# A new written-out order for all engines of a fused attention and squared-ReLU kernel, with load gates and PSUM banks named in the list

## The chip, the core and the metric

The kernel runs on one core of one Trainium2 chip. The metric is the device time of one execution in microseconds (us), as the median of the runs shown. The core has TensorE (PE in the profile, with its weight loads listed apart as PEld), VectorE (DVE), ScalarE (ACT), GpSimd (POOL) and SyncE (SP). Here POOL's instructions are nearly all starts of loads that convert float32 to float16 on the way, and SP's are starts of DMA transposes and of stores.

## The reference

Four batches of eight heads, 768 positions, head size 64, go through an attention in which each position sees eight global positions and the last 96 ones, with a distance bias. The result, 3072 tokens of 512 numbers, goes through a two-layer network with a squared ReLU.

```python
scores = scale * np.matmul(q, k.transpose(0, 1, 3, 2))
is_global = pos[None, :] < int(n_global)                 # n_global = 8
is_local = (rel >= 0) & (rel < int(n_local))             # n_local = 96
dist = np.where(is_global & ~is_local, float(n_local), np.abs(rel).astype(np.float32))
scores = scores + (-slopes[:, None, None] * dist[None, :, :])
scores = np.where(is_global | is_local, scores, -1000000000.0)
...
a = a / (np.sum(a, axis=-1, keepdims=True) + 1e-09)
x = np.matmul(a, v).transpose(0, 2, 1, 3).reshape(B * S, H * D)
h = np.maximum(x @ w_in, 0.0)                            # w_in 512 x 2048
out = h * h @ w_out                                      # w_out 2048 x 512
```

## The kernel before

**Tiling.** The tokens are cut into eight halves of 384 (three tiles of 128); half 0 and half 1 belong to batch 0, and so on. The heads go in four pairs, a = 0 to 3. Everything between the loads and the stores is float16, with float32 sums in PSUM, which has eight banks of 128 x 512.

**Attention.** For each half, q and k come in as tokens x features (`sq`, `sk`), are turned so that features lie on the partitions, and scored (`score_unit`, L691 holds its matmuls: 64 rows of weights, 128 columns). ACT takes the exponential (L704), DVE multiplies by a mask that holds bias and window (`weigh`, L728), PE multiplies with v (`attend`, L752; the 65th column gives the sum of the weights), and DVE divides (`norm`, L762, result `tm`). `tm` is turned into `xt`, features x tokens. For halves 0 and 1, "the opening", that work goes tile by tile and the turning is done by PE; half 2's q and k are turned by PE (`turn`, L629). For halves 3 to 7 SP turns q and k by DMA transposes (`turn_by_dma`, L647), and for halves 2 to 7 it turns `tm` into `xt` by four more, one for each pair (`to_x_by_dma`, L777).

**The network.** Layer 1 goes plainly over output tiles of 128 (`layer1`, L797), or, for part of the hidden width of halves 2 to 7, in groups of seven products of half size in place of eight (`layer1_group`, L900). These use sums and differences of quarters of w_in (`in_mix`) and of `xt` (`x_mix`, DVE, L878), and keep partial sums out of PSUM for a while (`hold`, a copy by ACT or DVE, printed as L336 or L338) to add them to later products (L958). ReLU and square follow on ACT or DVE (L822 and L836, L966 to L1000). Layer 2 goes plainly (`layer2`, L1052) or, for most of the tokens, two token tiles at a time in seven products (`layer2_pair`, L1138), with mixed weights `w_mix` and mixed hidden tiles `mixed` (`token_sum`, DVE, L1103). Its products share two or three PSUM banks named "a", "f" and "c". A product that adds to a bank waits until the copy (`hold`) or the hand-out (`hand_out`, L1200) of the bank's former content is done. Each pair's two rows of the output are stored by SP, 256 KB at a time; the last pair's last row is stored in pieces by SP and ACT.

**Loads.** POOL starts 128 KB loads of q, k and v tiles (L472), and 512 KB loads of quarters of w_in (L534) and of w_out (L541). No more than eight of its loads are outstanding in the trace. For halves 2 and up the loads of q and k into the staging tiles wait until the half before has been turned. For halves above 3, the first load of k is also placed behind both turning transposes of the half before, through a manual dependence (`behind`).

**The order.** The functions above only append operations to lists of `Plan`: PE's jobs (index p), loads (index l) and everything else (index a, d, s or g in the order, one common numbering). A job of p is a whole group of matmuls, such as one product or one score unit. The order in which all operations are then issued is the string `ORDER`, read by `by_table`: each word is a letter for the engine (p PE, l POOL's loads, a ACT, d DVE, s SP, g POOL) and an index. The same operation can stand as a or d, if both engines can do it. An engine works its words off in the order of the string, and waits where the data or the buffer of an instruction isn't ready. `run` also holds a small model of the engines' times. By it, it picks the PSUM bank of each PE job (the idle bank that came free first, `idle_banks`), and it works out how many filler matmuls on zeros stand ahead of some jobs in the first 24 us (`warm`, `spare`).

Of the kernel before, what the change touches and what calls it, by code (L numbers as in the profile page):

```python
# [41 lines left out]
AFTER = [0, 0, 0, 0, 0, 0, 0, 0]  # L42
# [10 lines left out]
ORDER = """d1 g2 a4 p0 a6 s8 d12 a0 s10 d17 l3 d13 l1 a18 a16 a19 l2 d21 d20 a27 l5 a26 d14 a22 d15 d3 a28 d5  # L53
p10 l4 a25 d9 p5 a30 d146 l0 a24 p1 a11 p2 d7 l6 a23 p3 l10 a32 d31 a33 d34 p6 l9 a29 d36 p7 a39 p11
d35 l7 p8 a46 p4 d43 p9 a41 l8 d37 p13 d44 a40 p12 d45 a47 l11 p14 d38 p16 a42 p15 d48 l13 p17 d51
a49 p19 p24 a52 l12 d55 p20 d64 p22 a50 p23 d58 l14 a53 p34 d56 p30 a60 p25 d71 p28 l16 p21 a81 d59
p26 d57 a82 l18 p27 d69 d67 p31 a65 d68 p18 a61 p29 l15 d72 p36 p32 a54 d70 p35 l19 a86 d66 p33 a73
d85 p39 d62 p40 l17 a74 a77 d76 p37 l21 d91 a78 p41 l20 d79 d63 p38 d83 l23 a101 d75 d84 p45 l22 a89
a87 d96 p44 l27 p47 a92 d80 p48 d107 a97 l29 d111 p46 a98 p52 l28 p43 a93 d110 p53 p42 d105 l30 d119
p55 d120 p50 l24 p59 a122 a88 d90 d99 a102 p51 l25 d106 a103 d94 p49 a116 a128 d108 p67 d100 a129  # L60
d95 a117 d112 p57 a104 p65 d125 p54 p58 d121 d189 p63 p61 p62 a132 d126 a109 p60 a114 d135 d118 a113
d115 p56 a127 d205 d191 a133 p74 a130 p72 a169 d138 p73 a165 d131 p77 d123 a166 p69 a167 p75 d156
d147 a157 p70 p71 d134 a158 p82 d159 l34 a162 d168 p81 a163 d186 l26 a170 p83 a142 p68 l31 d174 a139
d160 d149 p84 l35 a184 a164 d208 p64 a187 d124 l33 d161 a171 d148 a144 p85 l32 d272 a143 d206 p88
d207 l36 p89 d201 p79 d151 p86 a198 a178 d204 p91 d152 a195 a199 d188 p76 d202 a136 d150 p87 a172
d200 a179 p90 a196 d180 a193 p80 d153 a209 p78 s194 l37 p66 d155 a175 d203 a137 p95 d210 p92 a176
d223 a173 p94 d197 s224 l38 a185 d177 p100 a211 l39 d236 a181 s216 p93 a140 d237 p96 a182 p103 d238
s217 p97 d183 a244 a240 d221 a141 p102 d219 a222 d154 p106 s220 d213 d225 p98 p104 d239 s226 p99
d227 d228 p105 a234 d214 s229 d145 a218 d243 p101 l44 d245 d246 p107 l43 s215 d212 a241 d190 p109
l40 p110 p108 p111 a255 d192 l42 a251 p112 a256 d258 l45 a248 d257 p113 l41 a249 d230 d232 a252 p118  # L70
d259 p114 a273 d253 s260 l46 p116 d254 p115 a261 p120 d231 d250 l47 a262 p122 a264 p124 l48 s235
d280 p123 a265 d263 p131 a268 d233 a283 p127 d281 p126 a288 p132 d285 a269 p134 d295 s328 a287 p129
d270 a286 p119 a291 p142 d266 a293 p140 d296 s329 d314 p130 a311 p135 d267 a299 p128 d315 a292 p137
d274 a312 p136 d300 s242 p121 a305 s282 d327 a302 p125 a306 d289 p138 s275 a284 d303 p141 a307 d301
d304 a276 p117 d294 s290 a313 d308 p133 a271 l50 p139 d330 a278 p143 d297 a309 l56 p145 d279 a316
s298 p146 d310 p147 l53 a317 p144 d405 a334 l51 d322 p148 a326 a337 d323 l52 p149 a335 d443 d340
a331 l49 p151 d324 a341 p150 a332 d336 p152 l54 a342 d318 d325 p157 a348 p153 a343 d333 a345 d344
p159 p156 a346 d320 d319 a354 d407 p158 a356 p161 d321 a338 p172 d355 a359 p154 d349 p162 d377 a351
p169 p163 d360 a372 s378 l57 p164 d363 p167 a361 p166 d365 p171 d347 a368 p177 s408 a369 p160 d339
p165 a364 p170 a362 d357 p178 s409 l55 d373 a386 p175 a366 p173 a387 d382 p180 a367 p174 d376 p182  # L80
d374 p176 a379 s247 d383 p155 d380 s277 a384 s358 p179 d391 a385 p181 d395 a375 p168 s381 d353 d410
a393 p183 l58 a352 p184 d388 a370 a397 d394 l65 s396 p185 a392 d389 a399 d371 l62 p187 a398 d390
p188 p186 a419 l59 p189 d411 a415 a423 d412 l63 p190 a420 d426 a416 p191 d422 l73 a424 d414 a417
p192 l61 d421 a428 d425 p193 p194 p196 a432 l60 d413 a427 d418 a429 p198 p195 a436 d406 a444 d401
a433 p200 d492 p199 d402 a437 d447 p207 a430 p210 d435 a457 p204 s448 d445 p215 a462 p211 d453 p202
s350 d463 s446 p197 d439 a451 p203 d403 a464 p218 d496 d404 p206 a442 d441 d505 a475 d493 p205 a465
d438 p208 s507 p219 a455 d434 p213 a476 p201 d468 s508 a454 d431 a458 p223 p222 a472 d497 p214 a484
d469 d452 p217 a449 p212 s400 d470 a474 p209 d482 a456 p220 p227 d459 a477 s483 d466 p224 a500 p216
d495 a478 s467 l64 p221 d498 a471 p241 d479 a486 p225 l70 p229 a509 d488 d494 l66 p226 a489 d473
p228 a511 d490 a539 l69 d480 p231 d481 p233 l72 p230 a513 d501 d487 a519 l67 d460 p234 a520 d499  # L90
a512 l71 s440 p248 d521 a485 s506 d503 p235 l68 a514 d502 d522 a546 d510 p247 a461 d491 p236 s523
l74 d524 p237 a545 p232 d515 p239 a525 d531 a516 p246 d504 a517 p256 d544 p245 a536 p270 a528 d561
s537 d543 p240 a529 p249 d518 a538 p267 a547 d530 p251 a580 p255 d550 p252 a526 s595 p258 d559 a562
p243 a551 p266 d527 p238 a585 d578 s450 a553 p253 a565 d591 p254 s579 d541 a535 d554 p261 a557 p257
d532 s560 a568 p268 a558 d533 p242 a582 d555 s596 d563 a552 p260 d534 p250 a581 p269 d548 p264 p244
a567 a586 d574 p263 d542 a564 p259 d572 p262 a540 a583 p265 d556 p272 a575 s573 a597 d566 p271 d600
s549 d569 p277 d598 a576 d584 a599 p273 d570 a577 p274 d571 p275 p276 a601 d613 a608 d615 s614 l75
p278 a602 s593 d589 d616 a609 p279 a619 d617 s594 a604 p283 d587 a620 s592 d603 a611 a605 p281 d618
a631 p280 p282 a624 d588 p286 d606 a628 a625 p284 d634 a629 p287 d610 p292 a636 p288 d607 a632 d627
a635 d686 p294 a621 p301 d630 a646 p291 d637 d643 p299 d657 a641 p314 d626 a622 p290 d680 p285 d640  # L100
p307 s681 a633 p305 d623 p300 a665 p295 d655 s642 p293 s612 d647 d590 p296 d668 a644 p298 a656 d648
p309 a658 p289 d649 p308 a670 d654 p297 p304 d638 a651 p311 d652 s639 a663 p312 p306 d669 p317 d687
s653 p310 d688 a690 p302 d676 p316 p320 a684 s677 a650 p303 a685 d674 p328 p319 d671 a662 d666 a697
a672 p313 d659 p315 d696 p331 a675 d682 p318 a660 d691 d667 d678 a719 p333 a661 p332 d689 p321 d692
a664 d683 p335 d695 a716 p352 d698 d705 s699 p347 d693 s645 p334 d742 a752 p322 d723 a722 d673 p337
# [22 lines left out]
class Buffer:  # L128

    def __init__(self, tag, count):  # L130
        self.tag, self.count, self.users, self.taken = tag, count, [], False
# [7 lines left out]
class Plan:  # L139
# [51 lines left out]
    def free_at(self, op):  # L191
        t = self.last_move if op.move else 0.0
        for buf in op.bufs:
# [3 lines left out]
            if not buf.taken and len(ring) >= buf.count:  # L197
                for u in ring[-buf.count].users:
                    if u.done is None:
                        return None  # L200
# [1478 lines left out]
```

## Time and profile before

| | |
|---|---|
| three runs | 201.07, 200.97, 201.06 us, median 201.06 us |
| profiled execution: span of the instructions | 200.348 us |
| first matmul, first layer-1 product, end of the last group of products | 1.19, 20.04, 197.37 us |
| last copy out of PSUM (ACT), its store issued, landed | 197.39, 197.69, 199.39 us |
| matmuls | 2346 |
| DMA moved | 27.52 MB |

How to read it: a row of the chain of waits gives the start, the length, the engine, the tile and the line, with the number of instructions that run on from each other. A row of a group by lines gives the line, the engine, the operation, the tile written and those read, the size and the count, then the busy time and the mean of one in ns, then idle time ahead of it with what ended it. Matmuls overlap each other in PE's pipeline, so that a group's mean is longer than the step from one matmul to the next. A row of the timeline has a start, the length of a run of like instructions, and in brackets the idle time of the engine before it with what ended it. DMA issues are listed with their size and the median time from issue to landing.

### The profile page before, as it was taken

What the parts mean: (1) busy time and instruction counts of PE and PEld (TensorE: products, weight loads), DVE (VectorE), ACT (ScalarE), POOL (GpSimd) and SP (SyncE); (2) the same over time, 40 slices, a digit from 0 to 9 for tenths busy, and PEclk for the clock granted to TensorE, in tenths of its full rate; (3) what the DMA queues carried; (4) which work ended last, traced back from release to release, by engine and by line L of the source; (5) the groups of instructions that cost most, each with busy time, mean ns of one, the idle gap of its engine ahead of it and who ended that gap; (6) DMA issues with size and microseconds to landing.
All of it is one profiled execution on the core that took longest, in us unless ns stands there. A gap on an engine that the chain in (4) does not pass through costs nothing.

```text
span 200.3 us, 5912 instructions
## 1 busy us (share of the span) xinstructions
PE 193.0 (96%) x2346; PEld 161.3 (81%) x2346; DVE 178.9 (89%) x457; ACT 155.9 (78%) x335; POOL 66.7 (33%) x82
## 2 busy tenths in 40 slices
PE   7798999999999899999999999999999999999994
PEld 2685899766897587779878798899888988899993
DVE  7688698899999799989999999999989979998881
ACT  5999676898946889988999798989996669457411
POOL 8996564087108602920095019400000000000000
PEclk9999999999999999999999999999999999999999
DMA  5999999999999999999999989995230330210214
GB/s 154 180 150 197 187 181 173 209 192 154 176 203 74 141 206 219 120 115 99 221 133 147 155 203 144 166 246 111 53 114 3 124 61 3 105 56 0 108 52 157
DMA packets 106987, 27.52 MB, mean 137 GB/s; under 512 B 97104, under 2 KB 104016, under 8 KB 106960
## 3 DMA queue, kind: packets, MB, share of 16 engines
q0 software_dynamic: 74944, 13.11, 93.3%
q1 hardware_dynamic: 30816, 13.45, 30.9%
q10 hardware_dynamic: 1200, 0.59, 1.1%
q8 instruction: 18, 0.29, 0.6%
q14 instruction: 9, 0.07, 0.1%
HBM read 27.26 MB, written 6.29 MB: 167 GB/s over the span
## 4 chain that ended last, share of the span: by engine, by line
PE 72%; DVE 12%; DMA 7%; POOL 3%; ACT 2%; issue 1%; DVEq 0%; POOLq 0%
PE yps L1138 28%; PE hps L797 17%; PE hps L900 17%; DMA w_in_sb<-in_moe_w_in_dram 4%; PE sp L691 3%; PE av L752 3%; DMA xt<-tm 3%; PE yps L1052 2%; DVE phat L728 2%; POOL w_mix L472 2%; DVE tm L762 2%; POOL v L472 1%; ACT ex L704 1%; DVE hr L958 1%; DVE mixed L1103 1%
## 5 line engine op out<-in xcount | busy, mean ns | idle before, releaser
L797 PE MATMUL hps<-xt,w_in_sb 128*128 128x384 f16 (+2 forms) x336 | 45.1, 280 | 0.2 <-DMA w_in_sb<-in_moe_w_in_dram 0.2
L704 ACT ACTIVATE ex<-sp 128x512 f16<-128x512 f32 x66 | 36.4, 632 | 2.6 <-PE sp L691 2.5
L1138 PEld LDWEIGHTS <-h 128*128 128x128 f16 x376 | 34.3, 98 | 5.1 <-DVE h L838 0.2
L797 PEld LDWEIGHTS <-w_in_sb 128*128 128x128 f16 x336 | 28.1, 98 | 7.9 <-DMA w_in_sb<-in_moe_w_in_dram 0.7
L336 ACT COPY y<-yps 128x256 f32<-128x256 f32 (+2 forms) x42 | 15.5, 389 | 17.5 <-PE yps L1138 17.3
L1138 PEld LDWEIGHTS <-mixed 128*128 128x128 f16 x272 | 25.1, 98 | 3.7 <-DVE mixed L1103 0.6
L958 DVE TENSOR_TENSOR hr<-hps,kept 128x384 f16<-128x384 f32 x49 | 25.6, 551 | 2.2 <-ACT h L998 1.1
L472 POOL DMA_DIRECT2D sq<-in_q_dram x19 | 17.2, 907 | 29.7 <-DMA q<-sq 21.6
L336 ACT COPY kept<-hps 128x384 f32<-128x384 f32 x45 | 21.1, 490 | 7.4 <-PE hps L900 4.9
L822 ACT ACTIVATE hr<-hps 128x384 f16<-128x384 f32 (+1 forms) x44 | 22.2, 530 | 4.9 <-PE hps L797 4.8
L472 POOL DMA_DIRECT2D sk<-in_k_dram x19 | 17.1, 901 | 25.3 <-DMA q<-sq 13.6
L900 PEld LDWEIGHTS <-in_mix 128*128 128x128 f16 x272 | 23.0, 98 | 2.3 <-DVE x_mix L878 0.6
L900 PE MATMUL hps<-x_mix,in_mix 128*128 128x192 f16 x204 | 23.4, 246 | 0.3 <-ACT ex L704 0.3
L1138 PE MATMUL yps<-w_out_sb,h 128*128 128x256 f16 (+1 forms) x184 | 22.5, 268 | 0.1
L1138 PE MATMUL yps<-w_mix,mixed 128*128 128x256 f16 (+1 forms) x184 | 22.4, 268 | 0.1
L1138 PE MATMUL yps<-w_mix,h 128*128 128x256 f16 (+1 forms) x192 | 22.4, 264 | 0.0
L472 POOL DMA_DIRECT2D v<-in_v_dram x24 | 21.5, 908 | 2.6 <-DMA w_mix<-in_q_dram 0.9
L728 DVE TENSOR_TENSOR phat<-ex,mask 128x1024 f16<-128x1024 f16 (+1 forms) x36 | 20.7, 598 | 0.0
L900 PEld LDWEIGHTS <-w_in_sb 128*128 128x128 f16 x204 | 17.4, 98 | 2.1 <-issue 0.7
L900 PE MATMUL hps<-xt,w_in_sb 128*128 128x192 f16 x136 | 16.1, 246 | 0.5 <-DMA xt<-tm 0.5
L998 ACT ACTIVATE h<-hr 128x768 f16<-128x768 f16 x19 | 15.9, 853 | 0.4 <-DVE hr L968 0.3
L836 ACT ACTIVATE h<-hr 128x512 f16<-128x512 f16 (+1 forms) x22 | 15.9, 742 | 0.1
(115 smaller groups left out, 363.4 us busy)
## 6 DMA issues: line engine op xcount, KB each, us to landing
out_dram<-y SPq DMA_DIRECT2D x23, 256.0 KB, 2.5
v<-in_v_dram POOLq DMA_DIRECT2D x24, 128.0 KB, 6.8
sq<-in_q_dram POOLq DMA_DIRECT2D x19, 128.0 KB, 6.7
sk<-in_k_dram POOLq DMA_DIRECT2D x19, 128.0 KB, 6.7
w_in_sb<-in_moe_w_in_dram POOLq DMA_DIRECT2D x4, 512.0 KB, 10.9
w_out_sb<-in_moe_w_out_dram POOLq DMA_DIRECT2D x4, 512.0 KB, 12.3
y<-in_q_dram SPq DMA_DIRECT2D x2, 256.0 KB, 4.4
y<-in_k_dram ACTq DMA_DIRECT2D x2, 256.0 KB, 5.1
```

What stands on the lines that cost most here:

```text
L336: nc.scalar.copy(out=out, in_=in_)
L472: dma = nc.gpsimd.dma_start(out=dst, in_=src[x.b, :, r0 + t * P:r0 + (t + 1) * P, :] .rearrange("h p d -> p h d"))
L691: nc.tensor.matmul(sp[h][:, i, :], lhsT=lhsT, rhs=x.q[rows, r % HT, a, :], start=True, stop=True)
L704: nc.scalar.activation(out=st["ex"][:, h], in_=sp[h], func=AF.Exp, scale=scale)
L728: eng(e).tensor_tensor(out=x.phat[a][:, :, t0:t0 + n], op=ALU.mult, in0=st["ex"][:, :, i0:i0 + 2 * n].rearrange("p e (t b) c -> p e t (b c ...
L797: nc.tensor.matmul(st["ps"][:, i * n:(i + 1) * n], lhsT=w_in_sb[:, kk, m * P:(m + 1) * P], rhs=x.xt[:, kk, c0:c1], start=kk == 0, stop=kk ...
L822: nc.scalar.activation(out=o, in_=i, func=AF.Relu)
L836: nc.scalar.activation(out=h2, in_=hr, func=AF.Square)
L900: nc.tensor.matmul(st[name][:, i * HC:(i + 1) * HC], lhsT=left(i, kk), rhs=right(kk), start=fresh and i == kk == 0, stop=kk == KK - 1, ski ...
L958: eng(e).tensor_tensor(out=hidden(which)[:, :, cols], in0=sums(name), in1=st[kept], op=ALU.add)
L998: nc.scalar.activation(out=h2, in_=hr, func=AF.Square)
L1138: nc.tensor.matmul(st[bank_name][:, 0:n], lhsT=a(m), rhs=b(m)[:, cols], start=fresh and m == 0, stop=m == HK - 1, skip_group_check=not fresh)
```

## The change

The operations and what they compute stay as they are. What changes:

1. `ORDER` is another list. 61 operations move from ACT to DVE and 52 from DVE to ACT, and all engines' lists are in a new order. PE's runs of score products are cut in other places: before, it goes into such a run 17 times (5 of them ahead of the first layer-1 product), now 22 times (8 ahead of it).
2. A word has more in it: `p10.12+134` is PE's job 10, on PSUM banks 1 and 2, with fillers for 1.34 us; `l43@220` is load 43, placed by `behind` behind the operation with index 220. There are 21 words with such a gate, all on loads of halves 4 to 7. The former gate on the first load of k and that of the turning transposes on the last load of q are gone. So is the model of the engines' times, whose only use was to name the banks and the fillers. The fillers become 6 x 512 columns ahead of p10, 1 x 260 ahead of p14, 3 x 260 ahead of p27 and 3 x 128 ahead of p36, in place of 1 x 512, 3 x 260 (p27) and 2 x 512 (p37); 2353 matmuls in all.
3. The needs of some operations are finer: the loads of `sk` wait for the turning of k only, those of `sq` for that of q; the turning of k waits for the k loads alone, and that of q for the q loads alone. The PE turnings of batch 0 and of half 2 name the batch's buffers as a need.
4. The last PE jobs, before p365 p366 p367 p371 p361 p369 p370 p363 p372 p373, become p366 p367 p360 p370 p361 p369 p373 p371 p372 p363. The last one is then 256 columns wide (before, two of 128 columns end the list), and the row that it ends goes out in one store of 256 KB on SP.

Around the attention output of half 2, SP's transposes of pairs 0, 1 and 2 are the words s220, s229 and s226. Before they stood in the order s220, s226, s229, now s220, s229, s226; s215 (pair 3) comes later in both. DVE's division for pair 1 is d228; it stood behind d213, d239 and d227, and now stands ahead of them.

```diff
 ORDER
-... p98 p104 d239 s226 p99 d227 d228 p105 a234 d214 s229 d145 a218 d243 p101 l44 d245 d246 p107 l43 s215 ...
+... p104 d228 p99 d245 d190 p105.1 s229 a234 d227 d243 p107 d272 d239 s226 l43@220 p110.20 d246 ... l40@229 ...
...
-... s773 p361 d778 p369 s795 d774 p370 d791 p363 d792 s793 p372 a784 p373 d796 s785 s797 a798 a799
+... p361 d777 d792 d772 p369 p373 d791 d774 p371 s793 a798 s773 a799 p372 d794 p363 d796 s795 s797 a784 s785
...
     def run(self):
-        order = []
-        self.in_rows = False
-        for e, op in self.by_table() if ORDER else self.by_rank():
-            start = max(self.ready(op), self.free.get(e, 0.0))
...
-            taken = self.idle_banks(op.takes) if op.takes else []
...
-            self.now = [i for _, i in taken]
-            if taken and start < self.warm_until:
-                self.spare = start - 0.1 - max(idle, taken[-1][0])
-                self.spare *= 0.5 if start < self.warm_from + 5.0 else 1.0
-            self.take(op, start)
-            op.emit(e)
+        lists = {"p": self.queues["PE"], "l": self.queues["LOAD"]}
+        for word in ORDER.split():
+            word, _, spare = word.partition("+")
+            word, _, banks = word.partition(".")
+            word, _, gate = word.partition("@")
+            op = lists.get(word[0], self.rest)[int(word[1:])]
+            self.now, self.spare = [int(i) for i in banks], int(spare or 0) / 100
+            op.result = op.emit("POOL" if word[0] == "l" else self.LETTERS[word[0]])
+            if gate:
+                self.behind(op.result, self.rest[int(gate)].result)
...
     def list_loads(x, first=None):
-        before = (prev.turned if prev else []) + (halves[x.hb - 1].turned if x.hb > 2 else [])
...
+        if x.hb > 3:
+            before = {"sk": halves[x.hb - 1].turned[:1], "sq": halves[x.hb - 1].turned[1:]}
+        else:
+            last = halves[x.hb - 1].turned if x.hb > 2 else prev.turned if prev else []
+            before = {"sk": last, "sq": last}
...
-                if x.hb > 3 and name == "sk" and t == 0:
-                    for turn in halves[x.hb - 1].turns + (prev.xturns if AFTER[x.hb] else []):
-                        behind(dma, turn)
-                if name == "sq":
-                    x.last_load = dma
+                return dma
...
     def turn_by_dma(x):
-                if not x.turns:
-                    behind(turn, x.last_load)
                 x.turns.append(turn)
-            op = plan.add({"SP": 2.0 if i else 1.5}, emit, [*x.k_in, *x.q_in, x.bt.op, *late],
+                return turn
+            op = plan.add({"SP": 2.0 if i else 1.5}, emit, [*loads, x.bt.op, *late],
                           move=plan.TURN)
```

More of the change, by code (lines that the diff above doesn't have):

```diff
@@ L58 @@
[L58 to L62, printed above, removed]
@@ L149, with __init__ @@
     TURN, X_TURN, STORE, FIX = (0.2, 1.75, 0.6), (0.3, 1.1, 0.6), (0.45, 0.55, 0.8), (0.4, 0.5, 0.8)
-    def __init__(self, warm_from, warm_until):
-        self.warm_from, self.warm_until = warm_from, warm_until
+    def __init__(self):
         self.queues = {"PE": [], "LOAD": []}
         self.rest = []
-        self.free = {e: 0.75 for e in ("ACT", "DVE", "POOL", "SP")}
-        self.landed, self.last_move = 5.65, 0.0
         self.rank = 0
-        self.banks = [[] for _ in range(8)]
-        self.rings = {}
         self.first = []
+        self.now, self.spare, self.behind = [], 0.0, None
     def pe(self, cost, emit, needs=(), takes=0, lag=0.15, rows=False):
```

219 lines of the change are left out of this document (79 added, 140 removed).

## The prediction

> **What bounds the kernel now.** I read the page first, then the busy time of the stretch from 20 to 196 us, the chain of waits, and the matmul groups by shape.
>
> ```profile
> span 200.3 us, 5912 instructions
> PE 193.0 (96%) x2346; PEld 161.3 (81%) x2346; DVE 178.9 (89%) x457; ACT 155.9 (78%) x335; POOL 66.7 (33%) x82
> ```
> ```profile
> 20.00:196.00 176.00, 174.86 (x2086) 148.71 (x2087) 162.54 (x402) 138.23 (x297) 49.51 (x57) 1.00 1.22 134
> ```
>
> In the second fence the columns after the stretch's length are busy PE, PE weight load, DVE, ACT, POOL, then granted clock, DMA share and GB/s. PE looks full (174.86 of 176.00 us, clock 1.00), with DVE second at 162.54. But matmul ends are modelled, so short waits hide inside "busy". To find them I compare the work with the time it took. Work is counted by shape (first and last of 24 groups from 20 us on) and priced by rows of the chain in which PE ran unhindered.
>
> ```profile
> L797 PE MATMUL hps<-xt,w_in_sb 128*128 128x384 f16 x144 | 28.0, 326 | 0.0
> ...
> L1138 PE MATMUL yps<-w_mix,mixed 128*128 128x128 f16 x16 | 1.1, 219 | 0.0
> ```
> ```profile
> 11.57 8.42 DMA w_in_sb<-in_moe_w_in_dram
> 20.04 3.69 PE hps L797 x40
> 26.11 0.89 PE hps L797 x16
> 42.71 0.86 PE yps L1052 x4
> 84.90 0.55 PE sp L691 x16
> 94.37 0.65 PE hps L797 x4
> 96.04 0.61 PE av L752 x20
> 109.02 1.65 PE hps L900 x20
> 140.84 2.62 PE yps L1138 x24
> 143.46 0.78 PE sp L691 x24
> 148.62 0.98 PE yps L1138 x8
> 185.05 12.32 PE yps L1138 x144
> ```
>
> By width: 384 columns 0.65/4 = 0.1625 us, 144 of them, 23.4; 192 columns 1.65/20, 476, 39.3; 256 columns 2.62/24, 680, 74.2; 512 columns 0.86/4, 32, 6.9; 128 columns 0.89/16, 196, 10.9; 65 columns 0.61/20, 312, 9.5. The score products (64 rows) cost (0.78 - 0.55)/8 = 0.029 each, 264, 7.6. Each entry into a run of score products costs a fixed 0.55 - 16 x 0.029 = 0.09, and the first eight products behind it take 0.98 instead of 8 x 2.62/24 = 0.87: 0.20 in all, 12 entries, 2.4. Sum 174.2 us. It took from 20.04 to 185.05 + 12.32 = 197.37, which is 177.3. So PE waits **3.1 us** after its first layer-1 product; that product waits for the weights (11.57 + 8.42 = 19.99). A mere reordering can win little more than these 3.1 us. Two places hold 1.3 of them:
>
> ```profile
> 66.88 0.25 PE L900 MATMUL hps<-xt,w_in_sb 128*128 128x192 f16 x1
> 67.64 0.41 PE L900 MATMUL hps<-xt,w_in_sb 128*128 128x192 f16 x3 [0.52 <-DMA xt<-tm]
> ```
> ```profile
> 88.67 0.63 PE L900 MATMUL hps<-xt,w_in_sb 128*128 128x192 f16 x4
> 89.63 0.50 PE L900 MATMUL hps<-x_mix,in_mix 128*128 128x192 f16 x4 [0.33 <-ACT ex L704]
> ```
>
> One product took 67.64 - 66.88 = 0.76 instead of 0.08: a wait of 0.68 for the transposed attention output xt of half 2. Four took 89.63 - 88.67 = 0.96 instead of 0.33: 0.63, for xt of half 3 and for a PSUM copy that ACT did late. The other 1.8 us are a dozen waits of 0.05 to 0.25.
>
> **The change part by part.**
>
> *The order around the two big waits.* These rows are the stretch before the first one: the chain, and the three transposes that SP issues.
>
> ```profile
> 59.53 0.60 DVE h L1103
> 60.13 0.34 DVE y L1200
> ...
> 61.78 5.83 DMA xt<-tm
> ```
> ```profile
> 58.06 4.92 SPq L777 DMA_TRANSPOSE xt<-tm  x3
> ```
>
> The late transpose is the third of SP's three, that of pair 1: issued at 61.78, landed 5.83 later. In the new order DVE normalises pair 1 before two pieces that it did first here (0.60 + 0.34 = 0.94 us), SP issues pair 1 before pair 2 (a third of 4.92, 1.6 us), and three of half 4's loads are gated behind the transposes of pairs 0 and 1. It should land 0.9 to 2.5 us earlier, against a wait of 0.68: **-0.68**. What is late next is pair 2, now last; but no product reads it before the one that needs the mixed token tile, 1.9 us of products later.
>
> ```profile
> DMA to landing us min/median/max: 3.1/4.3/7.5
> ```
> ```profile
> 78.70 0.88 POOL L472 DMA_DIRECT2D sk<-in_k_dram  x1 [10.10 <-DMA k<-sk]
> ...
> 84.77 1.81 POOL L472 DMA_DIRECT2D v<-in_v_dram  x2
> ```
>
> The first row here is of the xt transposes from 50 to 95 us. Half 3's land while the nine loads of half 5 run, which POOL starts from 78.70 to 86.58; the slowest takes 7.5 us, the quickest 3.1. The new order gates seven of the nine, four of them behind the landing of half 3's first or third transpose and three behind later work. At the median the last one comes 3 us sooner. **-0.63**; bounds 0 (the ACT copy alone was the cause) and -0.63. The held loads arrive 2 to 4 us later; their cover is that their own turning (SP line 647) for half 5 now waits only for the k part and not for q as well.
>
> *Entries.* After the first layer-1 product the new PE list has 14 entries, not 12: **+0.4**. Before it there are 8 instead of 5, and 13 fillers instead of 6; that is covered by the weight transfer, since the load of the second quarter of w_in stays twelfth in POOL's queue and lands at 19.99. Bounds 0 to +0.6 (3 x 0.20): PE's list before it has little air left.
>
> *The end.* In the new order the last product is 256 columns wide, its row goes out whole through SP; before, two 128-column ones were last.
>
> ```profile
> 196.50 0.37 ACT L336 COPY y<-yps 128x256 f32<-128x256 f32 x1 [3.54 <-PE yps L1138]
> 197.39 0.27 ACT L336 COPY y<-yps 128x128 f32<-128x128 f32 x1 [0.52 <-PE yps L1138]
> ```
> ```profile
> out_dram<-y SPq DMA_DIRECT2D x1, 256.0 KB, 2.1
> ...
> out_dram<-y ACTq DMA_DIRECT2D x1, 64.0 KB, 1.7
> ```
>
> Copy 0.37 for 0.27, landing 2.1 for 1.7: **+0.5**, uncovered. Bounds +0.4 and +0.6.
>
> *Work between ACT and DVE.* 61 jobs go from ACT to DVE, 52 the other way.
>
> ```profile
> L1000 DVE TENSOR_TENSOR h<-hr 128x768 f16<-128x768 f16 x15 | 8.2, 553 | 0.2
> ```
> ```profile
> L998 ACT ACTIVATE h<-hr 128x768 f16<-128x768 f16 x19 | 15.9, 853 | 0.4 <-DVE hr L968 0.3
> ```
>
> A square costs 0.55 on DVE and 0.85 on ACT; the rows of the same kind price all 113. DVE gets 13 PSUM copies net (20 come, 7 go: +6.2), 14 squares for 15 (-0.4), fewer relus and their shares (-5.7), more copies of the opening and of the turnings (+3.8): +3.9 us, ACT -1.0. DVE's idle time from 20 to 196 us, 176.00 - 162.54 = 13.5, covers it: **0**, bounds 0 and, without the cover, +3.9.
>
> *One hand-over is shortened.*
>
> ```profile
> 101.26 0.23 PE L691 MATMUL sp<-q,k 64*128 64x128 f16 x2
> ...
> 102.04 1.05 PE L1138 MATMUL yps<-w_out_sb,h 128*128 128x256 f16 x8
> 103.07 1.70 PE L1138 MATMUL yps<-w_mix,mixed 128*128 128x256 f16 x14
> ```
>
> Three score units stand between the second and third product of one bank, and still the third starts late: its first eight products take 103.07 - 102.04 = 1.03, not 0.87, so 0.16 is lost. The new order leaves two units, 0.23 less cover: **+0.2**, bounds 0 and +0.4.
>
> *The small waits and the loads.* The remaining 1.6 us of small waits are re-dealt with the new bank numbers. I take a third off, **-0.5**; bounds -1.0 (some cadence error is in them) and +0.7. From 20 to 47 us loads land just as their products come up in the new list, and one 128 KB load has moved ahead of w_out: 0.88 us by the first of the load rows above. **+0.2**, bounds 0 and +0.5 (about half of that load uncovered).
>
> Sum: -0.68 - 0.63 + 0.4 + 0.5 + 0.2 - 0.5 + 0.2 = -0.5. The median of the runs is 201.06, 0.76 over the profiled span; that part (start and stop around the instructions) stays. 201.06 - 0.5 = **200.5**.
>
> **The rivals.**
>
> *A: more is won.* If the small waits shrink to what cadence errors leave (-1.0 instead of -0.5) and neither the hand-over nor the loads cost anything (-0.4): 200.5 - 0.5 - 0.4 = 199.6. For it: PE's list is full of places of 0.05 to 0.25 us, and a list laid out anew can close them. Against: prices must then hold to 0.05 us, and the landing times above spread by 4.4 us (3.1 to 7.5). Chance 0.18.
>
> *B: given back.* The two big waits go, but the re-dealt small ones stay at 1.6 us, on other instructions: 200.5 + 0.5 = 201.0. For it: the same spread. Chance 0.20.
>
> *C: DVE takes over, and it is slower.*
>
> ```profile
> 53.00:62.00 9.00, 9.00 (x103) 7.78 (x101) 8.69 (x21) 5.12 (x12) 1.33 (x2) 1.00 1.19 172
> 70.00:90.00 20.00, 19.53 (x239) 15.66 (x236) 18.81 (x48) 18.46 (x41) 7.88 (x9) 1.00 2.05 165
> 170.00:180.00 10.00, 10.00 (x100) 8.81 (x99) 9.45 (x25) 5.46 (x12) 0.00 (x0) 1.00 0.22 81
> ```
>
> Just where the late transposes are made, DVE has 9.00 - 8.69 = 0.3 us free, then 1.2 of 20. If it normalises pair 1 first, the two pieces it put off (0.94 us) become late for PE in their turn: the waits of 1.31 us change their name and stay, 201.8. Beside PE's work of 170 to 180 us the new list gives DVE 1.5 us more of durations than the old one, and 0.55 is free: up to 0.95 on top, 202.8. I take **202.2**. It decides from the point where DVE has under 0.3 us of idle time in one of these stretches. For it: DVE is the second engine by 13.5 us only, and the change adds to it. Against: from 70 to 90 us the new list gives it no more than the old, and most of its late jobs are not read at once. Chance 0.28.
>
> [...] Chance 0.04. [...]
>
> **How the numbers follow.** Forecast 0.30, A 0.18, B 0.20, C 0.28, D 0.04. A measurement of this kernel tells about 0.2% (0.4 us) from no change, so faster is below 200.66 and slower above 201.46. The forecast's own range is 199.6 to 201.2 (the bounds of the entries, the hand-over and half the small waits, not all at once). Faster: all but a sliver of A (0.17), two thirds of the forecast (0.20), a fifth of B (0.04): 0.41. Slower: nearly all of C (0.27), a little of B, D and the forecast (0.06): 0.33. Same: 0.26. The range leaves out the far ends of A and C: 199.3 to 202.5.
>
> **What would show it.** The transposes of half 2 in the order 0, 1, 2, with the second landed before 66.3 us, and no product of half 2 that takes over 0.2 us; the last transpose of half 3 landed in under 5 us, and no wait for it near 89. After the first layer-1 product, which should again start between 20.0 and 20.6, 14 entries into score products. At the end a copy of 256 columns at 0.37 and a 256 KB store as the last event, 2.1 us after its issue. DVE busy up by 3 to 4 us; if PE's waits name DVE or ACT where they named the transposes, C is right. A later first layer-1 product (by over 0.6), or waits for half 4's or half 5's turned q and k near 90 to 125 us (the gates), would make the prediction wrong in a way that none of the cases has.

## The result and the profile after

The changed kernel takes 211.47 us (median of four runs, 210.63 to 211.85) where the kernel before takes 201.06 (with a fourth run of 203.75): the ratio is 1.049, with an interval of 1.042 to 1.055. Times are medians of all runs, while ratios, here and below, leave out the slow ones, over 1.5% above the fastest of the same kernel. The profiled execution has a span of 209.9 us, 9.6 more than before.

The page's first part and the granted clock of its second part, after:

```profile
span 209.9 us, 5920 instructions
PE 195.0 (93%) x2353; PEld 162.2 (77%) x2353; DVE 180.4 (86%) x470; ACT 155.8 (74%) x322; POOL 66.5 (32%) x82
...
PEclk9999999999999999969999999999999999999999
```

The engines have hardly more to do: DVE is busy 1.5 us more, and PE 2.0 us more, part of which are fillers and matmuls at a slow clock. One slice has a clock of 0.6, which no slice had before. Here is who waited on PE (in total, times, longest one):

```profile
PE yps L1058 <- DVE mixed L1023: 4.0, 1, 4.0
PE hps L717 <- DMA xt<-tm: 2.5, 1, 2.5
PE hps L717 <- DMA w_in_sb<-in_moe_w_in_dram: 1.6, 2, 0.9
```

The same in time, from the timeline of PE, and the clock of 90 to 94 us:

```profile
21.46 2.81 PE L717 MATMUL hps<-xt,w_in_sb 128*128 128x256 f16 x32 [0.68 <-DMA w_in_sb<-in_moe_w_in_dram]
25.20 1.05 PE L717 MATMUL hps<-xt,w_in_sb 128*128 128x256 f16 x8 [0.93 <-DMA w_in_sb<-in_moe_w_in_dram]
```
```profile
90.51 0.82 PE L1058 MATMUL yps<-w_mix,mixed 128*128 128x256 f16 x3 [4.04 <-DVE mixed L1023]
```
```profile
136.01 0.48 PE L717 MATMUL hps<-xt,w_in_sb 128*128 128x384 f16 x2 [2.50 <-DMA xt<-tm]
```
```profile
90.00:94.00 4.00, 3.49 (x29) 2.36 (x30) 3.46 (x7) 0.60 (x2) 4.00 (x5) 0.57 1.42 90
```
```profile
199.90 6.62 PE yps L1058 x84
```

By the prediction's own count, the work behind the first layer-1 product is 174.2 + 0.4 for two more entries = 174.6 us. It ended at 199.90 + 6.62 = 206.52 and took 206.52 - 21.46 = 185.1, so PE loses 10.5 us there where it lost 3.1. That is +7.4; the first product is 21.46 - 20.04 = 1.4 later, the entries are 0.4, and from PE's end to the span's end there are 3.4 us, 0.4 more than before. Together 9.6. Of the 10.5, 9.1 stand in four rows: 0.9 for a quarter of w_in, 4.0 at 86 us, (1 - 0.57) x 4 = 1.7 for a clock at half speed right behind it, and 2.5 at 133 us.

**Where the 1.4 and the 0.9 come from.** POOL's timeline at the start of the changed order, the memset of v on DVE there, and the same two rows before:

```profile
6.71 1.02 POOL L396 DMA_DIRECT2D v<-in_v_dram  x1 [1.67 <-DVE sq L258]
...
12.91 1.56 POOL L454 DMA_DIRECT2D w_in_sb<-in_moe_w_in_dram  x2
```
```profile
6.31 0.10 DVE L405 MEMSET v<- 128x48 f16 x1
```
```profile
5.41 1.84 POOL L472 DMA_DIRECT2D v<-in_v_dram  x2 [0.31 <-DVE v L485]
```
```profile
5.00 0.10 DVE L485 MEMSET v<- 128x48 f16 x1
```

The first load of v goes into a tile that DVE fills with a column of ones first (the memset d3). In the new list d3 stands behind casts (sq and sk, L258), the first of which waits for its own data, so POOL stands still for 1.67 us and every load behind it is late: the weights are issued at 12.91, not at 11.57, though they stand at the same place in POOL's queue.

**Where the 4.0 come from.** POOL, DVE and the chain of waits around 86 us, and last POOL's row of half 4's v before:

```profile
70.83 1.80 POOL L396 DMA_DIRECT2D v<-in_v_dram  x2
80.70 0.88 POOL L396 DMA_DIRECT2D sk<-in_k_dram  x1 [8.07 <-DMA k<-sk]
81.57 0.89 POOL L396 DMA_DIRECT2D v<-in_v_dram  x1
88.89 0.88 POOL L396 DMA_DIRECT2D v<-in_v_dram  x1 [6.43 <-DMA xt<-tm]
```
```profile
84.36 0.68 DVE L1023 TENSOR_TENSOR mixed<-h 128x1024 f16<-128x1024 f16 x1
88.93 0.93 DVE L258 COPY vb<-v 128x520 f16<-128x520 f16 x2 [3.89 <-DMA v<-in_v_dram]
```
```profile
81.57 7.34 DMA v<-in_v_dram
```
```profile
65.94 2.65 POOL L472 DMA_DIRECT2D v<-in_v_dram  x3
```

Read upward from PE. Its product waits for a mixed tile; that tile's token sum stands in DVE's queue behind a copy of v (vb); the copy waits 3.89 us for the last v load of half 4 (l48), which landed at 81.57 + 7.34 = 88.91. POOL was free for it at 70.83 + 1.80 = 72.6, and before it started the three loads of half 4's v in one go; but in the new list it stands behind l50, a load of half 5's k, which has the gate @328 and in any case writes the tile that SP is still turning. So one load that must wait holds one that need not, through three queues.

**The 2.5 at 133 us** are for xt of half 5, pair 2: a row of the chain says that it was issued at 128.81 and landed 7.16 us later; POOL had begun another burst of loads at 127.07.

### The profile page after: what moved, and what is told of

Read it like the earlier page. It is cut to its first block, busy times and chain, and to the rows that moved or that the text cites. A ratio compares the mean times of both kernels' runs of the same rounds, so it can differ in the third digit from the quotient of the medians.

```text
span 209.9 us, 5920 instructions
## 1 busy us (share of the span) xinstructions
PE 195.0 (93%) x2353; PEld 162.2 (77%) x2353; DVE 180.4 (86%) x470; ACT 155.8 (74%) x322; POOL 66.5 (32%) x82
## 4 chain that ended last, share of the span: by engine, by line
PE 47%; DMA 31%; DVE 13%; POOL 5%; issue 2%; ACT 0%; POOLq 0%; SPq 0%; DVEq 0%
PE yps L1058 23%; PE hps L820 16%; DMA v<-in_v_dram 10%; DMA w_out_sb<-in_moe_w_out_dram 6%; DMA xt<-tm 5%; PE hps L717 5%; DMA w_in_sb<-in_moe_w_in_dram 4%; DMA k<-sk 3%; DMA sk<-in_k_dram 2%; PE av L671 2%; DMA y<-in_q_dram 2%; DVE mixed L1023 2%; POOL w_mix L396 2%; PE sp L610 2%; DVE w_mix L488 2%
## 5 line engine op out<-in xcount | busy, mean ns | idle before, releaser
L623 ACT ACTIVATE ex<-sp 128x512 f16<-128x512 f32 x66 | 35.8, 625 | 8.6 <-PE sp L610 8.3
L1058 PEld LDWEIGHTS <-mixed 128*128 128x128 f16 x272 | 25.6, 99 | 8.0 <-DVE mixed L1023 4.6
L742 ACT ACTIVATE hr<-hps 128x384 f16<-128x384 f32 (+1 forms) x47 | 23.9, 539 | 4.2 <-PE hps L717 4.0
L1058 PE MATMUL yps<-w_mix,mixed 128*128 128x256 f16 (+1 forms) x184 | 23.0, 274 | 4.1 <-DVE mixed L1023 4.0
L256 ACT COPY y<-yps 128x256 f32<-128x256 f32 (+2 forms) x34 | 13.0, 394 | 17.5 <-PE yps L1058 17.5
L820 PE MATMUL hps<-x_mix,in_mix 128*128 128x192 f16 x204 | 24.2, 246 | 0.0
L256 ACT COPY kept<-hps 128x384 f32<-128x384 f32 x39 | 18.1, 486 | 7.5 <-PE hps L820 6.2
L918 ACT ACTIVATE h<-hr 128x768 f16<-128x768 f16 x21 | 17.7, 856 | 0.0
L756 ACT ACTIVATE h<-hr 128x512 f16<-128x512 f16 (+1 forms) x21 | 15.2, 741 | 1.2 <-DVE hr L744 1.0
```

Source lines behind the costliest of these rows:

```text
L256: nc.scalar.copy(out=out, in_=in_)
L623: nc.scalar.activation(out=st["ex"][:, h], in_=sp[h], func=AF.Exp, scale=scale)
L742: nc.scalar.activation(out=o, in_=i, func=AF.Relu)
L756: nc.scalar.activation(out=h2, in_=hr, func=AF.Square)
L820: nc.tensor.matmul(st[name][:, i * HC:(i + 1) * HC], lhsT=left(i, kk), rhs=right(kk), start=fresh and i == kk == 0, stop=kk == KK - 1, ski ...
L918: nc.scalar.activation(out=h2, in_=hr, func=AF.Square)
```

## The experiments

These kernels ran on other chips or at other times than the first measurement, each beside runs of the kernel before, which took 200.0 to 205.3 us there. The ratio is to those runs; it says more than the time, and two kernels are told apart only where their intervals lie apart.

| kernel | us | ratio | interval |
|---|---|---|---|
| old_order_new_code | 202.58 | 0.9995 | 0.994 to 1.005 |
| before_v48_late | 203.23 | 1.010 | 1.006 to 1.015 |
| before_memset_late | 206.80 | 1.024 | 1.017 to 1.032 |
| before_pair1_first | 203.88 | 0.998 | 0.990 to 1.007 |
| after_again | 209.69 | 1.031 | 1.022 to 1.040 |
| v48_first | 208.64 | 1.033 | 1.024 to 1.043 |
| memset_first | 208.82 | 1.038 | 1.033 to 1.042 |
| gate328_off | 208.42 | 1.034 | 1.026 to 1.041 |
| two_moved | 211.50 | 1.041 | 1.033 to 1.050 |
| no_gates | 214.48 | 1.056 | 1.048 to 1.065 |
| two_moved_no_gates | 211.76 | 1.044 | 1.036 to 1.051 |
| gate467 | 214.49 | 1.062 | 1.053 to 1.071 |
| six_behind_467 | 215.02 | 1.057 | 1.045 to 1.068 |
| three_mended | 211.61 | 1.039 | 1.025 to 1.052 |
| four_mended | 211.50 | 1.041 | 1.032 to 1.050 |
| five_mended | 210.43 | 1.043 | 1.030 to 1.056 |
| fillers_in_waits | 207.66 | 1.027 | 1.018 to 1.036 |

### The list or the code

```diff
 # changed kernel's code, ORDER = the former list, banks and fillers written out
+... p10.12+33 ... l40@217 ... l49@329 ... l58@409 ... l67@508 ...
```

> The changed kernel's code with the former list in it: the same order on every engine, the same PSUM banks and number of fillers written out, the finer needs, and four gates in place of the former ones (the first load of k of halves 4 to 7 behind the turning of the half before). Order theory: the list alone is what costs, and the time is that of the kernel before within 1 us. Rival, the code (finer needs, banks named in the list, gates by word) costs by itself: over 2 us more than before.

The ratio is 0.9995. The finer needs, the banks in the list and the new way to gate cost nothing that these runs tell under the former list (0.994 to 1.005), so the loss comes with the new order and its gates.

### Single words of the former order

```diff
 # before_v48_late
-... l47 a262 p122 a264 p124 l48 s235 ... a271 l50 p139 ...
+... l47 a262 p122 a264 p124 s235 ... a271 l50 l48 p139 ...
 # before_memset_late
-... d14 a22 d15 d3 a28 d5 p10 l4 a25 d9 p5 a30 d146 l0 a24 p1 a11 p2 d7 l6 ...
+... d14 a22 d15 a28 d5 p10 a25 d9 p5 a30 d146 a24 p1 a11 p2 d7 d3 l4 l0 l6 ...
 # before_pair1_first
-... s220 d213 d225 p98 p104 d239 s226 p99 d227 d228 p105 a234 d214 s229 ...
+... s220 d213 d225 p98 d228 p104 d239 s229 s226 p99 d227 p105 a234 d214 ...
```

> The former order with one word moved: l48 behind l50, as in the changed one (PSUM banks 2 and 3 change places from there on, for the model in the kernel names them anew). Queue theory: l48 starts near 79.6 us and lands near 85 instead of at 75.9, DVE stands still from 82.3 until then (2.9 us), and the time grows by 1.5 to 3.5 us, to 202.6 to 204.6. Rival: DVE's jobs behind it have air, and the time grows by less than 0.6.

> The former order with DVE's memset d3 behind the cast d7, and the first two loads of v behind it (up to three fillers change their number, by the model in the kernel). Queue theory: the first load of v starts near 7.7 us instead of 5.4, all loads behind it shift, the first layer-1 product starts near 22.2 instead of 20.0, and the time grows by 1.5 to 3 us. Rival: later air takes it up, under 0.7 us.

> The former order with two words moved: DVE's division for pair 1 of half 2 (d228) right behind the product p98 that feeds it, and its transpose s229 ahead of s226. The prediction's first term: the transpose lands before 66.5 us and PE's wait of 0.68 at 66.9 us goes; 0.3 to 0.7 us less than the kernel before, which these runs hardly tell from none (ratio 0.995 to 1.002). Rival: the pieces that DVE puts off (token sum, hand-out) are late in their turn, and a new wait of 0.5 us or more stands near 61 us.

Moving l48 brings PE's wait of the changed kernel into the former order:

```profile
PE yps L1139 <- DVE mixed L1104: 3.6, 1, 3.6
```

The time grows by 1.0%, some 2 us and less than the wait. The trace is of an execution of 206.59 us, though, and how long PE waits in one of the median 203.23 is not shown. The memset's place costs more than was expected, 2.4%. POOL and PE of that kernel:

```profile
7.77 1.75 POOL L472 DMA_DIRECT2D v<-in_v_dram  x2 [2.67 <-DVE v L485]
```
```profile
21.98 2.27 PE L797 MATMUL hps<-xt,w_in_sb 128*128 128x128 f16 x27 [0.87 <-DMA w_in_sb<-in_moe_w_in_dram]
```

The loads are 7.77 - 5.41 = 2.4 us late, the first layer-1 product 21.98 - 20.04 = 1.9; the rest is lost later, most of it in two waits for xt, 2.4 us in all, from 87.3 and 90.7 us on. So both places found in the trace of the changed kernel are a cost by themselves in the former order. The third edit is the prediction's first term alone. It does what was said: the transposes of half 2 land in 3.2 to 4.7 us, the one of pair 1 ahead of its reader, and PE's wait at 67 us is gone, with no new wait near 61. Its worth, forecast at 0.3 to 0.7 us, can't be told from none (0.998).

### Single words of the changed order

```diff
 # v48_first
-... l50@328 ... l48 ...
+... l48 l50@328 ...
 # memset_first
-... d13 l3 ... d14 ... d3 p10.12+134 l4 ...
+... d13 d3 l3 ... d14 ... p10.12+134 l4 ...
 # gate328_off
-... l50@328 ...
+... l50 ...
```

> The changed order as it is, on the same chip as the three below, as their reference. The first two runs of single moved words took 208.6 and 208.8 us beside a kernel before of 200.0 to 205.0, so that chips or hours differ: 209.5 to 212.5 us expected, with PE's waits at 86 us (3 to 4.5 us) and near 133 us (1.5 to 3 us).

> The changed order with one word moved: load l48 (v, last tile of half 4) stands ahead of the gated load l50 instead of behind it. Queue theory: POOL starts l48 right behind l46, near 72.6 us, it lands before 82 instead of at 88.9, DVE's vb copy r405 no longer waits, and PE's wait of 4.2 us at 86 goes together with the stretch of slow clock behind it: 205 to 206.5 us instead of 211.5. Rival, DVE has become the bound: it is late there anyway, and the time stays over 210.

> The changed order with one word moved: DVE's memset d3 (the column of ones of batch 0's v) stands right behind d13 instead of behind the casts. Queue theory: the first load of v starts near 5.05 us instead of 6.71, the second quarter of w_in lands near 19.9 instead of 21.4 and the first at 23.6 instead of 25.2: 1.4 to 2.5 us are won, 209.0 to 210.1. Rival, the opening has air later on: PE's wait at 86 us grows by what is won, and the time stays at 211.1 to 211.8.

> The changed order with the gate of load l50 on the turning of half 4's k taken off, nothing moved. Place theory: l50 writes the staging tile that this turning reads, so that it waits for the same landing without the gate; l48 is as late as before, 211.1 to 211.9 us. Gate theory: the added gate itself holds POOL, and without it the wait at 86 us goes: 205 to 207.

With 208.4 to 208.8 us these three are not told apart from the changed order on another chip (after_again, 209.69), so no gain in time is shown for any of them; v48_first was expected at 205 to 206.5. The traces tell more. In v48_first the wait at 86 us is gone, but PE now waits 1.2 us for half 5's turned q, 2.0 for DVE's weighting behind it, and 3.3 for xt of half 5. In gate328_off POOL's row for the load without its gate reads:

```profile
79.69 0.88 POOL L395 DMA_DIRECT2D sk<-in_k_dram  x1 [8.11 <-DMA k<-sk]
```

It waits for the same landing as with the gate (80.70 and 8.07 in the changed kernel): the place in the queue holds l48, not the gate. So the place theory holds in the trace; the time, 208.4, came out some 3 us under what was expected, but is not told apart from the unchanged list's 209.7 on another chip.

### Several at once

```diff
 # two_moved: v48_first and memset_first together
 # no_gates: all 21 gates off; two_moved_no_gates: both
-... l43@220 ... l50@328 ... l75@573 ...
+... l43 ... l50 ... l75 ...
```

> The changed order with both words moved: l48 ahead of l50, and the memset d3 right behind d13. Queue theory: both prices are won, but the gates that are left hold POOL behind SP's transposes still, so that waits for turned q and k near 100 us and for xt near 130 us remain: 205 to 207 us. Rival, the two words were all: 201 to 203 us.

> The changed order with all 21 gates on loads taken off, nothing moved. Queue theory with the gates as the larger part: POOL starts half 5's loads from 80.5 us on in one go and not from 88.9, l48 stays behind l50 and costs 2 to 4 us, the waits near 100 and 130 us shrink: 206.5 to 209 us. Rival, the gates keep loads off the xt transposes and help: slower than the changed order by over 0.5 us.

> The changed order with both words moved and all 21 gates taken off. Queue theory: what holds POOL is gone but for its own buffers, and the order is worth about what it was before: 201 to 204 us, and under two_moved by 2 us or more. Rival, the gates were no cost: within 0.7 us of two_moved. If the prediction's terms hold for the rest of the order, it comes out near 201.

Here my theory of two prices that can be won back fell. two_moved takes 211.50, not 205 to 207, and two_moved_no_gates 211.76, not 201 to 204. Who waits on PE in it:

```profile
PE hps L716 <- DMA xt<-tm: 2.1, 1, 2.1
PE av L670 <- DVE phat L646: 1.4, 1, 1.4
PE sp L609 <- DMA q<-sq: 1.3, 1, 1.3
PE av L670 <- DMA v<-in_v_dram: 0.8, 1, 0.8
```

The wait of 4 us is gone, but 1.4 + 1.3 + 0.8 = 3.5 us for half 5's q and v have come, whose loads stand behind gates, and the 2.1 for xt of half 5 stay; the mean clock of 0.982 over 209.3 us is some 3.8 us lost to the clock, with no slow stretch ahead of 95 us. Without gates the order takes 214.48 us, not 206.5 to 209, and is slower than after_again beside it (1.056 to 1.031, intervals apart), so the rival held: the gates do earn something in it. With both words moved and no gates, xt meets the loads again, which POOL starts until 84.2 us: PE waits for xt three times, 5.6 us in all, the first time near 89 us.

### The transpose of half 5

```diff
 # gate467
-... l71@483 ... l64@483 ... l65@483 ... l69@483 ...
+... l71@467 ... l64@467 ... l65@467 ... l69@467 ...
 # six_behind_467: also
-... l74@508 ... l66@507 ... s467 ... l71@483 ...
+... s467 ... l74@467 l66@467 l71@467 ...
```

> The changed order with four gates moved on by one transpose: loads l71, l64, l65 and l69 behind s467 (xt of half 5, pair 2, the last of its four) instead of s483. Collision theory: with only two loads beside it, that transpose lands in 4 to 5 us instead of 7, and PE's wait near 131 us shrinks from 2.4 us to under 0.6, with the slow clock behind it gone where there was one: 2 to 4 us less than the changed order's 209.7 to 211.5, so 206 to 209. Rival, the transpose is slow by itself: the wait stays over 2 us.

> The changed order with six loads (l74, l66, l71, l64, l65, l69) behind s467, the last xt transpose of half 5, so that no load is started ahead of it. Refined collision theory: one load started before a transpose delays it as eight do (6.84 us with two, 6.55 with nine); with none it lands in 2.3 to 3 us, and PE's wait near 131 us (2.4 to 2.9 us) goes. The loads come later than in gate467 by nothing, so that the wait near 138 us for half 6's v, which gate467 showed, stays at 1 to 3 us: the total is 207 to 213. Rival: the transpose takes over 5 us all the same.

Landing of that transpose in gate467, where one load was started 0.6 us ahead of it, one 0.2 us behind it and no other, and in six_behind_467, where none was in flight (in both a store stands right ahead of it in SP's list; in gate467 it started 0.65 us before):

```profile
DMA to landing us min/median/max: 6.8/6.8/6.8
```
```profile
DMA to landing us min/median/max: 4.0/4.0/4.0
```

Here two loads delay it nearly as much as the whole burst (7.16 in the changed kernel); that refutes the theory of gate467, by which it would land in 4 to 5 us. The number does count elsewhere: the second transpose of half 3 takes some 5.7 us with one load beside it (v48_first: it was issued at 79.22, and POOL, which waited for it, went on at 85.23, by the changed kernel's rows 0.28 behind the landing) and 7.16 with two (the changed kernel), while the slowest of half 3 takes 7.5 with nine (the kernel before). With none this one takes 4.0, more than the 2.3 to 3 expected, and PE's wait for it goes; whether the store makes up the rest was not tried. But both kernels are slower than after_again and no quicker than the first measurement, for the loads that were put off held the next copy of v: six_behind_467 waits 4.8 us for x_mix at 138 us.

### Following the chain

```diff
 # three_mended: two_moved and six_behind_467
 # four_mended: and half 5's gates off
-... l50@328 ... l56@275 ... l49@290 ... l53@275 ... l51@275 ... l55@408 ... l57@409 ...
+... l50 ... l56 ... l49 ... l53 ... l51 ... l55 ... l57 ...
 # five_mended: and half 6's v where POOL is idle
-... l62@396 ... l74@467 l66@467 l71@467 ... l64@467 ... l65@467 ...
+... l62@396 l65 l64 l66 ... l74@467 l71@467 ...
```

> The changed order with l48 ahead of l50, the memset d3 behind d13, and the six loads behind s467. Chain theory: the waits at 86 and 131 us are gone, the one near 100 to 108 us (half 5's turned q, its v; 3.8 us and slow clock in two_moved) stays, as half 5's gates do: 207 to 211 us. Rival, the loss is spread: 211 or more, with no wait over 1 us.

> As three_mended, and half 5's seven gates off (l49, l50, l51, l53, l55, l56, l57). Chain theory: the waits from 100 to 108 us go; xt of half 3 meets half 5's loads again as it does in the former order (1 to 2.5 us near 88): 203.5 to 207 us, and under three_mended by over 2 us. Rival, those gates are not the place: within 1 us of three_mended.

> As four_mended, with the three loads of half 6's v (l64, l65, l66) right behind l62 without a gate, where POOL is idle from 113 to 129 us, and l74 alone of half 7's first loads left behind s467 with l71 and l69. Chain theory: these loads land before 123 us, DVE's vb copy no longer stands still at 132 us, PE's wait of 4.9 us at 133.7 goes with the slow clock behind it (3.4 us lost there), and xt of half 5 still lands in about 4 us: 203 to 206 us instead of 211.5, the former order's level within 2%. Rival, the loss is spread and moves on once more: 209 or more.

Each edit took away the wait that it was meant to, and the total stayed at 210 to 212 us. The chains that then set PE's longest wait, four_mended first:

```profile
132.92 4.82 DMA v<-in_v_dram
137.74 0.02 issue
137.76 0.57 DVE vb L257
138.33 0.27 DVE x_mix L797
```
```profile
113.84 11.62 DMA k<-sk
125.47 0.02 issue
125.49 0.36 DVE kb L256 x2
```

In four_mended it is the pattern of the 86 us place once more, with half 6's v. In five_mended those loads run from 112.80 on, while three of half 6's q are still under way, and the turning of half 6's k, issued at 113.84, takes 11.62 us beside them; DVE's copies wait for it, and PE waits 3.8 us for DVE. For the last two the chain theory foresaw 203.5 to 207 and 203 to 206 us: it fell, and the rivals held (four_mended within 1 us of three_mended; the loss moves on). Why this list has no place for these loads that hurts nobody stays open; a list in which they fit (the former one) differs in too many words.

### The clock

```diff
 # fillers_in_waits
-... p152 ... p248.3 ...
+... p152+260 ... p248.3+220 ...
+                for _ in range(int(plan.spare / 0.11)):
+                    nc.tensor.matmul(st[bank_name][0:16, 0:n], lhsT=zeros, rhs=w_out_sb[:, 0, 0:n],
+                                     start=False, stop=False, skip_group_check=True)
```

> The changed order with matmuls on zeros put into its two long waits of PE: 23 of 256 columns (2.5 us) ahead of p152, 10 of 512 columns (2.2 us) ahead of p248; they add zero to 16 rows of the bank or are overwritten. The waits end when they ended before. Clock theory: a wait of over some 2 us lets the granted clock fall to 0.50 for the next 3.4 us, and busy PE keeps it: the clock stays at 1.00 behind both places, and 1.7 us are won for each one that was slow, 1.5 to 3.5 us less than the changed order. Rival, the slow clock hangs on something else (power, time): it stays, and nothing is won.

The fillers in PE's timeline, the clock behind them (86 to 92 and 128 to 136 us), and for comparison the clock at the same places in after_again:

```profile
86.08 2.68 PE L1063 MATMUL yps<-w_out_sb,zeros 128*16 128x256 f16 x23
88.69 1.05 PE L1067 MATMUL yps<-w_mix,mixed 128*128 128x256 f16 x8
```
```profile
86.00:92.00 6.00, 6.00 (x68) 4.82 (x67) 4.82 (x11) 2.49 (x7) 4.81 (x6) 1.00 1.24 151
...
128.00:136.00 8.00, 8.00 (x80) 5.48 (x80) 6.18 (x15) 5.18 (x11) 7.01 (x8) 1.00 1.82 125
```
```profile
88.00:92.00 4.00, 4.00 (x37) 3.05 (x35) 3.01 (x7) 2.34 (x5) 3.55 (x5) 0.57 1.81 116
...
133.00:136.00 3.00, 3.00 (x16) 2.27 (x15) 0.26 (x2) 0.48 (x1) 1.29 (x2) 0.50 2.76 151
```

The tile of zeros is 128 x 16; ahead of p248 a like loop writes to the bank that its first real product overwrites. With zeros in the two waits the clock stays at 1.00, and this is the quickest of all kernels with the changed order. Its ratio of 1.027 is clear of the first measurement of the changed order (1.049) but not of the second (1.031), so that the trace shows that the clock stays up, and the size of the gain, 1.7 us for each slow stretch, is worked out from the clock.

## Why the prediction was wrong

**What bounds the kernel** was read rightly: PE has no idle time but 3.1 us. What I drew from it was one-sided. If PE has nearly no waits, a new order can hardly win, and every transfer that it makes late can lose; my range let it lose 1.4 us.

**The step that failed first** was that what stands ahead of the first layer-1 product "is covered by the weight transfer, since the load of the second quarter of w_in stays twelfth in POOL's queue and lands at 19.99". The place in the queue stayed; what the queue waits for did not. The memset on DVE that the fifth load needs had moved behind a cast that waits for data. The weights landed at 21.4, and the first layer-1 product came 1.4 us later, the next quarter of w_in cost 0.9 more. before_memset_late shows that such a shift costs by itself in the former order (+2.4%).

**The step that cost most** was the cover of the gated loads, "that their own turning (SP line 647) for half 5 now waits only for the k part and not for q as well". I followed the gated loads to their own readers. What counted were the ungated ones behind them in POOL's queue: l48 is half 4's, it stood ahead of l50 in the former order, and it feeds DVE, whose queue feeds PE: 4.0 us of waiting and 1.7 at a slow clock. before_v48_late shows the price by itself in the former order, +1.0%. The delay was also put far too low, at "2 to 4 us": the last two loads of half 5's v start at 104.83, where they started at 84.77.

```profile
104.83 1.82 POOL L396 DMA_DIRECT2D v<-in_v_dram  x2
```

In the changed kernel that cost PE nothing; with l48 ahead (two_moved) it comes to light as 3.5 us of waits. And the 2.5 us for xt of half 5 have no term at all: the meeting of transposes and loads was priced for half 3 alone. How much of the 10 us each step is worth in the new order stays open, as none of the mended lists there is shown to be quicker. The last paragraph of the prediction named "a later first layer-1 product" and waits behind the gates as what would make it wrong; a look at DVE's place of d3 and at POOL's order around l50, both in the lists, would have made them terms of the sum.

**Point by point.** The first term (-0.68) was right in its mechanism: SP's three transposes of half 2 went 0, 1, 2 and landed quickly, the products that read them did not wait.

```profile
DMA to landing us min/median/max: 2.4/2.8/3.8
```

The second (-0.63) was right in its effect, though not by its sign: half 3's slowest transpose landed in 7.16 us and not in under 5, but PE has no wait for it near 89. In the changed kernel the wait of 4.0 us may hide one; in v48_first and three_mended, which don't have that wait, none is listed from 76 to 95 us either. Where half 5's gates are off as well it is there, with 1.5 us for xt in two_moved_no_gates and 1.7 for x_mix, which is made of xt, in four_mended. The end came out at +0.4 for +0.5.

The hand-over (+0.2) was misread. The three score units ahead of the product at 102.04 stay three in the new list; the run that loses a unit is the next one. And what came late there was the product at 103.07, which reads a mixed tile. In the changed kernel the same eight products take 109.74 - 108.64 = 1.10, not 1.03, and the chain of waits names DVE's mixed tile, done at 109.69, as what the next product waited for; no bank is named:

```profile
108.64 1.05 PE L1058 MATMUL yps<-w_out_sb,h 128*128 128x256 f16 x8
109.74 1.92 PE L1058 MATMUL yps<-w_mix,mixed 128*128 128x256 f16 x16
```

DVE grew by 1.5 us, not 3 to 4; its PSUM copies, squares and relus came out about as reckoned, so the copies of the opening and the turnings were put too high.

**The rivals.** C has the right sign for another reason: the longest wait names DVE, but DVE itself stood idle for a load. From 20 to 205.5 us, about where PE's work ends now, DVE is free for 185.50 - 165.27 = 20.2 us, more than the 13.5 of the stretch to 196 before:

```profile
20.00:205.50 185.50, 177.25 (x2117) 150.14 (x2116) 165.27 (x418) 139.69 (x289) 49.44 (x57) 0.99 1.15 126
```

D, the case with a chance of 0.04, is shown by no run: once POOL may start, DVE's work does not show in its pace. In the changed kernel it starts the loads from 88.89 us on every 0.87 us, while DVE is busy for 4.50 of the 4.61 us to 93.50. None of the cases had a wait that moves through POOL, DVE and PE, and none had the clock.

## What to carry to other kernels

A queue that works in order passes a wait on to everything behind it (here l48, for which POOL was free at 72.6 us, started at 81.57): when a word moves in a list of loads, look at what stands behind the load that waits, and who reads that, not only at the load that was moved. Count what a new order can lose and not only what it can win; in this kernel, whose main engine was 96% busy, there were 3.1 us to win, and 10 were lost. When a mended place does not lower the time, look for where the wait has gone before looking for another cause.

## What the hardware showed that was not expected

**The clock.** After a long wait of PE the granted clock often falls to 0.50 for 3.4 us, a loss of 1.7 us: from 90.4 to 93.7 us in the changed kernel, from 88.3 to 91.7 in after_again, and once more there, from 132.6 to 136.0 us at least. It mostly falls between 0.3 us ahead of the wait's end (gate467, at 87.4 us) and 1.5 us behind it (old_order_new_code, at 91.0). In two kernels it falls 0.9 us or more before the wait's end and stays down for 6.8 us (memset_first, from 86.0 us on) or for 6.5 us at least (six_behind_467, from 88.5 us on). The wait's length alone does not decide: waits for xt of 2.3 us at 133 us in after_again and of 1.7 us at 89 us in old_order_new_code brought it, of 2.5 us at 133 us in the changed kernel and of 1.7 us at 91 us in before_memset_late did not. What does decide is not shown.

**Transposes beside loads.** SP's transposes land in 2.3 us at best (the changed kernel), in some 5.7 with one load of 128 KB started 0.8 us ahead (v48_first), in 6.8 and 7.2 with two started within a microsecond of them (gate467, the changed kernel at 81.45 us), in up to 7.5 beside the nine loads of half 5 (the kernel before), and once in 11.62, with six loads started in the 3.7 us ahead of it or within a microsecond behind it (five_mended). Two rows of the changed kernel, for two transposes of half 5 issued just ahead of POOL's burst and for the one issued 1.7 us into it:

```profile
DMA to landing us min/median/max: 2.3/2.3/2.4
```
```profile
DMA to landing us min/median/max: 7.2/7.2/7.2
```
